# Coarse keys as 126 + 18 from the second batch on: four transposes instead of six, the rest keys of three groups in one

## The chip, the cores and the metric

The kernel runs on one core of a Trainium2 chip. The metric is the device time of one launch in microseconds (us). A NeuronCore has five engines that run side by side, each through its own instructions in order: TensorE (PE in the profile, its weight loads PEld), VectorE (DVE), ScalarE (ACT), GpSimd (POOL) and SyncE (SP, which here only issues DMAs). PE reads SBUF and writes PSUM; ACT and DVE read PSUM; POOL can't. Each DMA is issued from an engine's instruction stream, here from SP or POOL, and an engine that waits before a DMA holds back all that stands behind it in its stream.

## The reference

Inputs q, k, v are [8 batches, 8 heads, 576 positions, 64], in fp32. Two attentions are added, and the sum goes through a gated convolution and an output matrix:

```
# coarse: every 4 neighbouring positions are averaged, 576 -> Sd = 144 queries and keys
q_d = q.reshape(B, H, Sd, factor, D).mean(axis=3)      # k_d, v_d alike
out_d = sm_attn(q_d, k_d, v_d)                         # softmax over all 144 coarse keys
out_up = np.repeat(out_d, factor, axis=2)
# local: softmax over |i - j| < 4
attn_out = out_up + out_local
# then x = attn_out as [8, 576, 512]:
gate_pre = sum over 5 taps of conv_w[k] * x shifted    # causal, per channel
out = (sigmoid(gate_pre) * (x @ w_val)) @ w_out
```

## The kernel before

The heads are taken in pairs, so there are 32 of them: pair p is batch p // 4 and head pair p % 4 (two heads of 64 fill 128 partitions). For each pair PE makes, by their names in the profile:

- `mk`, `sl`: the local scores of ten blocks of 58 queries (L719 adds the band mask, L732 makes 40 small products), then a softmax on DVE and ACT (`mx`, `ex`, `sm`, `rs`, `pexp`).
- `sd`: the coarse scores (L809). They lie as three groups of 48 queries, [112 rows, 3 groups, 144 keys], the two heads at rows 0 to 47 and 64 to 111. From pair 8 on the scores of two pairs are made at once. ACT makes the exponentials `pd` group by group (L832) with their sums, and one of DVE, POOL or ACT multiplies them by the reciprocal sums (L855 or L857).
- `tl0`, `tl1`: five transposes of the local weights (L889), copied by ACT to `pt`.
- `tc0`, `tc1`: transposes of the coarse weights (L912). The 144 keys are cut in two halves of 72, and for each half the three groups are transposed, [112 x 72] to [72 x 112], into one PSUM tile: six transposes a pair. ACT copies each PSUM tile to `pdt` (L919), 72 x 336 values, twice a pair.
- `x`: local weights times values (L939, 20 products).
- `odp`: coarse weights times values (L981). From pair 4 on four products: for each half of the keys and each head, 72 keys by 64 columns of `vs` against 144 columns of `pdt`. ACT copies the result to `od` (L991), and DVE adds x and od to `xt` (L950).

From `xt` come the split into high and low parts (`xhs`, `xls`), and five taps of the convolution: ACT makes the first (L1024) into a buffer `gp`, DVE the other four (L1030), ACT the gate (L1041). There are GB = 7 buffers `gp`; the next user of one waits for the product `h` (L1147) that reads it.

The projections `val` and `out` run over blocks of 504 columns (all 4608 positions in a row), each in products of three fp32r passes (L1119 to L1121). They are cut into pieces of three matmuls (six in the last two half blocks) that a list calls P; they fill PE between the steps of the pairs. Eight P go with each pair in the steady order

```
STEADY = "odp'' x'' sd tc1' tc0' P P P P mk sl tl1' tl0' P P P P"
```

where two strokes mean the pair two steps back, and one stroke the pair before. A planner in the kernel takes every step with a cost, its dependencies and its buffers, and writes from that the order of each engine's instructions; it may take a step of the list up to 14 places early. Where it expects PE to idle, it puts matmuls on constants (L592) ahead of a step, to keep PE's clock up.

Values for `odp`: the four positions that make one coarse key are summed by DMAs. In the first batch `vg` comes in whole, and PE adds the four. From the second batch on `vs` is loaded from SP (`vs0`), and three DMAs on POOL add the rest (`vs1` to `vs3`, L634), each waiting for the one before. One such set serves the four pairs of a batch; up to four sets are held. VROWS = 80 rows of 4 KB go in each, of which 72 hold keys. The summed queries and keys `qs` come the same way from the third batch on.

DMAs on SP go through `send` (L609), which lets the fifth wait until the first of five has landed (PACE = 4). Work can move between DVE and POOL (and for the coarse normalization also ACT): the planner picks whichever is free.

Of the kernel before, what the change touches and what calls it, by code (L numbers as in the profile page):

```python
# [55 lines left out]
GB = 7  # L56
# [116 lines left out]
class Planner:  # L173
# [106 lines left out]
    def simulate(self):  # L280
# [97 lines left out]
        while len(start) < len(ops):  # L378
# [12 lines left out]
            for e in engines:  # L391
# [27 lines left out]
                if e == "SP":  # L419
                    flight.append(k)  # L420
# [67 lines left out]
def tensor_order(np_):  # L488
# [41 lines left out]
def tile_two_scale_attn_gated_conv(  # L530
# [6 lines left out]
    vgr: bass.AP,  # L537
    w_val: bass.AP,
# [24 lines left out]
    ods = [cpool.tile([P, SQ // 2], F32, name=f"od{i}") for i in range(2)]  # L563
    xhs, xls = (cpool.tile([P, NC, spot(LASTB * S) + S], F32R, name=n) for n in ("xhs", "xls"))
# [58 lines left out]
    def sums_in(b):  # L623
        u = bt.setdefault(b, {})

        def first(nm, src, shape):
            def run():
                u[nm] = inp.tile(shape, F32, tag=nm, name=f"{nm}{b}", bufs=VSB if nm == "vs" else 2)
                send(out=u[nm], in_=src[b, 0])
            return run  # L630

        def more(nm, src, r):
            def run():
                nc.gpsimd.dma_start(out=u[nm], in_=src[b, r], accum_op=ALU.add)  # L634
            return run

        for nm, src, shape, user, size in (
            ("qs", qkr, [P, NC, 2, SD], "sd", P * NC * 2 * SD * 4),
            ("vs", vgr, [VROWS, NC, 4, D], "odp", VROWS * NC * 4 * D * 4),
# [149 lines left out]
    def coarse_scores(p):  # L789
# [37 lines left out]
        def exp(g):  # L827
            def run():
                if g == 0:
                    s["pd"] = work.tile([ROWS, NG, SD], F32, tag="pd", name=f"pd{p}")  # L830
                    s["csm"] = small.tile([ROWS, NG], F32, tag="csm", name=f"csm{p}")
                nc.scalar.activation(  # L832
                    out=s["pd"][:, g],
# [18 lines left out]
        def norm(eng):  # L852
            if eng is nc.scalar:
                for g in range(NG):
                    nc.scalar.mul(s["pd"][:, g], s["pd"][:, g], s["crs"][:, g : g + 1])  # L855
                return
            return eng.tensor_tensor(  # L857
                out=s["pd"], in0=s["pd"], in1=s["crs"].broadcast_to([ROWS, NG, SD]), op=ALU.mult
# [43 lines left out]
    def coarse_transpose(p, kb):  # L902
# [3 lines left out]
        def mm():  # L906
# [4 lines left out]
            for i in range(NG):  # L911
                nc.tensor.transpose(  # L912
                    out=tp[:, i],
                    in_=s["pd"][:, i, half * kb : half * kb + half],
# [3 lines left out]
        def evac():  # L918
            nc.scalar.copy(out=s["pdt"][:, kb], in_=s["tc", kb])  # L919

        op(
            (f"tc{kb}", p), "PE", 295, mm, [("cnorm", p)],
            banks=[("t", [(f"pdt{kb}", p)])], cols=(588, 336), loads=3,
        )
        op((f"pdt{kb}", p), "ACT", 335, evac, [(f"tc{kb}", p)], free=[("odp", p - 2)])
# [425 lines left out]
```

## Time and profile before

| what | value |
|---|---|
| runs | 372.8, 372.87, 376.79 us (median 372.87) |
| the profiled execution's own time | 373.75 us |
| its span, first to last instruction | 371.5 us |
| mean granted TensorE clock | 0.999 |
| PE busy | 358.9 us (97%) |
| DVE busy | 304.9 us (82%) |
| ACT busy | 247.5 us (67%) |
| POOL busy | 91.1 us (25%) |
| bytes moved by DMA | 68.97 MB |

Busy time of PE counts a matmul until its result is written, so that matmuls that follow each other overlap, and a busy PE can still be waiting for weights. What a step costs PE is read from where the next one starts. An fp32 product shows as two matmuls (two passes), a transpose as one. Line numbers are those of the kernel before.

### The profile page before, as it was taken

The page shows a single profiled execution, that of the slowest core. Times are in us where ns is not written, and L with a number is a line of the kernel's source. Part 1 is how long each engine was busy: PE and PEld are TensorE (multiplying, and loading weights), DVE is VectorE, ACT ScalarE, POOL GpSimd, SP SyncE. Part 2 cuts the span into 40 slices and gives each one's busy share as a digit, 9 for nine tenths or more (in the row PEclk, how much of TensorE's full clock was granted, in tenths as well). Part 3 has the DMA queues.
Part 4 walks back from the last instruction along what each step waited for, and adds up shares of the span by engine and source line. Part 5 has one row for each costly group of instructions (what it writes and reads, how often), then busy time and mean ns, then how long its engine had stood idle before and what let it go on. Part 6 is the DMA issues. An engine that isn't in the chain of part 4 may idle for free.

```text
span 371.5 us, 14101 instructions
## 1 busy us (share of the span) xinstructions
PE 358.9 (97%) x6020; PEld 286.0 (77%) x6020; DVE 304.9 (82%) x673; ACT 247.5 (67%) x664; POOL 91.1 (25%) x116
## 2 busy tenths in 40 slices
PE   7899899998999999999999999999999999999996
PEld 4677676776777777777778787777777778778996
DVE  3988999998999989997999799879997999570520
ACT  2898798967875949674777587857874767422221
POOL 4211225741462116102522052203100320000000
PEclk9999999999999999999999999999999999999999
DMA  7899999999989969995799879892345101102012
GB/s 248 246 278 297 332 220 231 268 249 292 285 187 275 255 197 235 200 280 199 197 207 232 279 187 203 228 239 68 101 154 160 37 3 59 56 0 85 28 49 79
DMA packets 23550, 68.97 MB, mean 186 GB/s; under 512 B 2880, under 2 KB 8768, under 8 KB 23488
## 3 DMA queue, kind: packets, MB, share of 16 engines
q1 hardware_dynamic: 18592, 50.42, 42.0%
q0 software_dynamic: 4608, 17.50, 26.0%
q8 instruction: 47, 0.77, 0.9%
q10 hardware_dynamic: 288, 0.16, 0.2%
q14 instruction: 15, 0.12, 0.1%
HBM read 58.63 MB, written 9.44 MB: 183 GB/s over the span
## 4 chain that ended last, share of the span: by engine, by line
PE 75%; DMA 11%; DVE 9%; ACT 3%; issue 2%; POOL 0%; SPq 0%; DVEq 0%; ACTq 0%
PE val L1119 8%; PE val L1121 8%; PE val L1120 8%; PE out L1119 8%; PE out L1120 8%; PE out L1121 8%; DMA vg<-in_vg 6%; PE x L939 5%; PE sl L732 5%; PE odp L981 5%; PE tl L889 5%; PE tc L912 4%; DMA qk<-in_qk 3%; DVE gp L1030 3%; PE sd L809 3%; DMA out_t<-ob 2%
## 5 line engine op out<-in xcount | busy, mean ns | idle before, releaser
L1030 DVE SCALAR_TENSOR_TENSOR gp<-xt,cw,gp 128x576 f32<-128x576 f32 x128 | 106.0, 836 | 2.6 <-ACT gp L1024 2.4
L1119 PE MATMUL val<-xhs,wh_v 128*128 128x504 f32 (+1 forms) x160 | 63.2, 395 | 0.0
L1121 PE MATMUL val<-xls,wh_v 128*128 128x504 f32 (+1 forms) x160 | 59.6, 372 | 0.1
L1120 PE MATMUL val<-xhs,wl_v 128*128 128x504 f32 (+1 forms) x160 | 59.5, 372 | 0.0
L1119 PE MATMUL out<-hhl,wh_o 128*128 128x504 f32 (+1 forms) x144 | 57.6, 400 | 0.1
L1121 PE MATMUL out<-hhl,wh_o 128*128 128x504 f32 (+1 forms) x144 | 54.8, 380 | 0.0
L1120 PE MATMUL out<-hhl,wl_o 128*128 128x504 f32 (+1 forms) x144 | 54.7, 380 | 0.0
L1147 DVE SCALAR_TENSOR_TENSOR h<-gp,val 128x288 f32<-128x288 f32 (+6 forms) x64 | 26.7, 447 | 18.8 <-PE val L1121 18.5
L1211 ACT ACTIVATE ob<-out 128x504 f32<-128x504 f32 (+2 forms) x40 | 22.0, 551 | 24.7 <-PE out L1121 11.4
L832 ACT ACTIVATE pd<-sd,cbi 112x144 f32<-112x144 f32 x96 | 35.4, 380 | 1.6 <-DVE cbi L825 1.6
L1121 PEld LDWEIGHTS val<-xls,wh_v 128*128 128x128 f32 x160 | 30.1, 188 | 5.6 <-DVE xls L1013 0.5
L1119 PEld LDWEIGHTS val<-xhs,wh_v 128*128 128x128 f32 x160 | 30.1, 188 | 4.1 <-issue 0.2
L1120 PEld LDWEIGHTS val<-xhs,wl_v 128*128 128x128 f32 x160 | 30.2, 189 | 3.5
L1119 PEld LDWEIGHTS out<-hhl,wh_o 128*128 128x128 f32 x144 | 27.2, 189 | 5.8 <-issue 1.0
L1167 POOL TENSOR_TENSOR hhl<-h,hhl 128x504 fp32r<-128x504 f32 x15 | 19.2, 1278 | 49.9 <-DVE gp L1030 23.6
L1024 ACT ACTIVATE gp<-xt,cw 128x576 f32<-128x576 f32 x32 | 24.8, 776 | 9.5 <-DVE h L1147 7.4
L1121 PEld LDWEIGHTS out<-hhl,wh_o 128*128 128x128 f32 x144 | 27.1, 188 | 5.1
L1120 PEld LDWEIGHTS out<-hhl,wl_o 128*128 128x128 f32 x144 | 27.2, 189 | 3.8
L732 PEld LDWEIGHTS sl<-qk 64*29 64x29 f32 x2560 | 24.8, 103 | 6.9 <-issue 1.6
L1161 ACT CAST hhl<-h 128x504 fp32r<-128x504 f32 (+2 forms) x44 | 22.1, 521 | 11.9 <-DVE h L1147 11.9
L1009 ACT CAST xhs<-xt 128x576 fp32r<-128x576 f32 (+4 forms) x40 | 22.3, 577 | 11.7 <-DVE xt L950 11.4
L950 DVE TENSOR_TENSOR xt<-x,od 128x290 f32<-128x290 f32 x64 | 26.3, 450 | 4.6 <-PE x L939 3.3
(96 smaller groups left out, 731.5 us busy)
## 6 DMA issues: line engine op xcount, KB each, us to landing
qk<-in_qk SPq DMA_DIRECT2D x31, 586.0 KB, 5.6
qs<-in_qkr POOLq DMA_DIRECT2D x18, 576.0 KB, 7.9
vw<-in_vw SPq DMA_DIRECT2D x32, 320.0 KB, 5.9
out_t<-ob SPq DMA_DIRECT2D x32, 252.0 KB, 5.2
vs<-in_vgr POOLq DMA_DIRECT2D x21, 320.0 KB, 7.5
qs<-in_qkr SPq DMA_DIRECT2D x6, 576.0 KB, 7.4
vs<-in_vgr SPq DMA_DIRECT2D x7, 320.0 KB, 5.4
raw_v<-in_w_val SPq DMA_DIRECT2D x4, 512.0 KB, 6.0
```

The source lines that it names most:

```text
L732: nc.tensor.matmul(out=sc[32 * qd : 32 * qd + BQ, b, m * KW : (m + 1) * KW], lhsT=t[r, 0, 3 + blk : 3 + blk + BQ], rhs=t[r, 1, blk : blk + ...
L832: nc.scalar.activation(out=s["pd"][:, g], in_=s["sd"][:, g], func=AF.Exp, scale=1.0 / 128.0, bias=s["bi"][:, g : g + 1], accum_out=s["csm" ...
L950: nc.vector.tensor_tensor(out=s["xt"][:, 4:].rearrange("p (m a j r) -> p a m j r", m=NPR, a=2, r=2)[:, par], in0=s["x"][par].rearrange("p ...
L1009: nc.scalar.copy(out=xhs[:, c, g : g + t - f], in_=s["xt"][:, 4 + f : 4 + t])
L1024: nc.scalar.activation(out=s["gp"], in_=s["xt"][:, 4 : 4 + S], func=AF.Copy, scale=cw[:, c, 4:5])
L1030: return nc.vector.scalar_tensor_tensor(out=s["gp"], in0=s["xt"][:, k : k + S], scalar=cw[:, c, k : k + 1], in1=s["gp"], op0=ALU.mult, op1 ...
L1119: nc.tensor.matmul(out=o, lhsT=wh[:, d, col], rhs=his[d], start=d == 0, stop=False)
L1120: nc.tensor.matmul(out=o, lhsT=wl[:, d, col], rhs=his[d], start=False, stop=False)
L1121: nc.tensor.matmul(out=o, lhsT=wh[:, d, col], rhs=los[d], start=False, stop=d == NC - 1)
L1147: nc.vector.scalar_tensor_tensor(out=t["h"][:, cs], in0=st[b * NC + c]["gp"][:, f:e], scalar=1.0, in1=box["o"][:, cs], op0=ALU.add, op1=AL ...
L1161: nc.scalar.copy(out=t["hh"][:, cuts[n]], in_=t["h"][:, cuts[n]])
L1211: nc.scalar.mul(t["ob"][:, cs], box["o"][:, cs], 0.5)
```

## The change

For pairs 4 to 31 (the second to the last batch):

- ACT writes the exponentials interleaved, `pd` is [112, 144 keys, 3 groups], so that neighbouring keys of a group lie 12 bytes apart.
- The keys are cut into KM = 126 and KR = 18. Three transposes take the first 126 keys of each group ([112 x 126], read with the 12 byte step), and a fourth takes the last 42 keys of all three groups together, which lie in one run of 126 numbers. One PSUM tile [126, 4, 112] holds all, and one ACT copy of 126 x 448 takes it to `pdt`. The steps `tc0` and `tc1` become one, `tc1`.
- `odp` is two products of 144 columns (one a head) over 126 keys, and six of 48 columns (one a group and head) over the fourth transpose. For these, `vz` holds for each group the values of the 18 rest keys in the rows where that group's weights lie; its other rows are zero.
- `vs` is loaded as 126 rows of 2 KB. The 18 rest keys `vr` come beside it, in four further DMAs a batch (one from SP, three adding ones on POOL). `vz` is filled for each pair by three DMAs on SP from `vr`, 18 rows of 512 bytes each, which wait for the last sum `vr3` and for `odp` of the pair two before. Two `vz` buffers are zeroed once on POOL.
- GB goes from 7 to 6.

The first batch keeps its cut of 72 and 72, but its `pd` is interleaved too.

```diff
+KM, KR = 126, 18
+KW3 = KM // 3
-GB = 7
+GB = 6
...
+    vzs = [cpool.tile([KM, NG, 2, D], F32, name=f"vz{i}") for i in range(2)]
...
+            ("vs", vgr, [KM, 2 * NC * P], "odp", KM * NC * P * 4),
+            ("vr", vrr, None, "odp", KR * NC * P * 4),
...
+    def spread(p):
+        b, c = divmod(p, NC)
+
+        def dma(i):
+            def run():
+                nc.sync.dma_start(
+                    out=vzs[p % 2][KM - NG * KR + i : KM : NG, i].rearrange("k h d -> k (h d)"),
+                    in_=bt[b]["vr"][:, P * c : P * c + P],
+                )
+            return run
+
+        for i in range(NG):
+            op((f"vz{i}", p), "SP", 620, dma(i), [("vr3", b), ("vzero", 0)], free=[("odp", p - 2)], size=KR * P * 4)
...
-                    s["pd"] = work.tile([ROWS, NG, SD], F32, tag="pd", name=f"pd{p}")
+                    s["pd"] = work.tile([ROWS, SD, NG], F32, tag="pd", name=f"pd{p}")
...
-                    out=s["pd"][:, g],
+                    out=s["pd"][:, :, g],
...
+        def mm4():
+            s["pdt"] = work.tile([KM, NG + 1, ROWS], F32, tag="pdt", name=f"pdt{p}")
+            s["tc"] = tp = ps.tile([KM, NG + 1, ROWS], F32, tag="t", name=f"tc{p}", bufs=TB)
+            keep_warm(tp.rearrange("p a b -> p (a b)"))
+            for i in range(NG):
+                nc.tensor.transpose(
+                    out=tp[:, i],
+                    in_=s["pd"][:, 0:KM, i],
+                    identity=(ident_s if crossed(p, i) else ident)[0:ROWS, 0:ROWS],
+                )
+            nc.tensor.transpose(out=tp[:, NG], in_=s["pd"][:, SD - KW3 :].rearrange("p k i -> p (k i)"), identity=ident[0:ROWS, 0:ROWS])
+
+        def evac4():
+            nc.scalar.copy(out=s["pdt"], in_=s["tc"])
...
+                for h, r in enumerate((LO, HI)):
+                    nc.tensor.matmul(
+                        out=od_ps[r].rearrange("p (i j) -> p i j", j=GR),
+                        lhsT=vd[:, h],
+                        rhs=s["pdt"][:, 0:NG, 64 * h : 64 * h + GR],
+                        start=True,
+                        stop=False,
+                    )
+                for i in range(NG):
+                    for h, r in enumerate((LO, HI)):
+                        x = 64 * (1 - h if crossed(p, i) else h)
+                        nc.tensor.matmul(
+                            out=od_ps[r, GR * i : GR * i + GR],
+                            lhsT=vzs[p % 2][:, i, h],
+                            rhs=s["pdt"][:, NG, x : x + GR],
+                            start=False,
+                            stop=i == NG - 1,
+                        )
```

The planner gets costs for the new steps and writes a new order for every engine.

On PE, in the middle of the run (pair 21; `odp`, `x` and `tc` as above, `val` and `out` are pieces of the projections), there stands before:

```order
L1121 MATMUL val_3_4148<-xls,wh_v 128x504
L981 MATMUL odp_4185<-pdt_4032,vs_2608 64x144 x4
L939 MATMUL x_4193<-pt_4135,vw_3685 64x58 x20
L912 MATMUL tc_1_4221<-ident_s,pd_4062 72x112
L912 MATMUL tc_1_4221<-ident,pd_4062 72x112 x2
L912 MATMUL tc_0_4228<-ident_s,pd_4062 72x112
L912 MATMUL tc_0_4228<-ident,pd_4062 72x112 x2
L1119 MATMUL out_0_4234<-hhl_0_3967,wh_o 128x504
```

and now, at the same place:

```order
L1186 MATMUL val_3_4229<-xls,wh_v 128x504
L1026 MATMUL odp_4268<-pdt_4130,vs_2459 64x144 x2
L1036 MATMUL odp_4268<-pdt_4130,vz_90 64x48 x6
L986 MATMUL x_4282<-pt_4216,vw_3793 64x58 x20
L951 MATMUL tc_4308<-ident_s,pd_4213 126x112
L951 MATMUL tc_4308<-ident,pd_4213 126x112 x2
L956 MATMUL tc_4308<-ident,pd_4213 126x112
L1184 MATMUL out_0_4320<-hhl_0_4058,wh_o 128x504
```

The steps stand as they stood; four products became two wide and six narrow ones, and six transposes became four.

On SP, where the values of the second batch are first needed (`qk_1138` and `qk_1220` belong to pair 8, `vw_1151` and `vw_1169` to pair 7, `vs_1039` and `vs_1043` to the third batch), there stands before:

```order
L609 DMA qs_957<-in_qkr 128x1152
L609 DMA vw_1011<-in_vw 128x640
L609 DMA vs_1039<-in_vgr 80x1024
L609 DMA qk_1138<-in_qk 128x1172
L609 DMA vw_1151<-in_vw 128x640
L609 DMA qk_1267<-in_qk 128x1172
L609 DMA vs_1287<-in_vgr 80x1024
L609 DMA vw_1344<-in_vw 128x640
L609 DMA qk_1397<-in_qk 128x1172
```

and now (`vz_89` and `vz_90` are the two `vz` buffers, and `vs_604` the second batch's values):

```order
L615 DMA vs_1043<-in_vgr 126x512
L615 DMA vs_1067<-in_vgr 126x512
L667 DMA vz_89<-vs_604 18x128
L615 DMA vw_1169<-in_vw 128x640
L667 DMA vz_89<-vs_604 18x128 x2
L667 DMA vz_90<-vs_604 18x128 x3
L615 DMA vs_1043<-in_vrr 18x512
L615 DMA qk_1220<-in_qk 128x1172
L615 DMA vs_1067<-in_vrr 18x512
L667 DMA vz_89<-vs_604 18x128 x3
L667 DMA vz_90<-vs_604 18x128 x3
L615 DMA qk_1380<-in_qk 128x1172
```

The loads of pair 8 and 9 (`qk_1220`, `qk_1380`) now stand behind the spreading DMAs of pairs 4 to 7.

On DVE, around the `xt` of pair 4 (`xt_85<-x_1117` before, `xt_85<-x_1134` now; `gp` are taps of pairs 2 and 3), there stands before:

```order
L821 TENSOR_REDUCE cmx_1192<-sd_1162 112x3
L950 TENSOR_TENSOR xt_85<-x_1117,od_87 128x5x58 x2
L825 TENSOR_SCALAR cbi_1210<-cmx_1192 112x3
L769 TENSOR_TENSOR pexp_81<-ex_83,rs_1187 64x2x5x35
L1030 SCALAR_TENSOR_TENSOR gp_851<-xt_86,cw,gp_851 128x576
L1030 SCALAR_TENSOR_TENSOR gp_1058<-xt_84,cw,gp_1058 128x576
```

and now:

```order
L846 TENSOR_REDUCE cmx_1203<-sd_1175 112x3
L794 TENSOR_TENSOR pexp_81<-ex_83,rs_1200 64x2x5x35 x2
L1165 TENSOR_TENSOR wl_o<-a_o_1128,wh_o 128x512
L1095 SCALAR_TENSOR_TENSOR gp_855<-xt_86,cw,gp_855 128x576
L1095 SCALAR_TENSOR_TENSOR gp_1063<-xt_84,cw,gp_1063 128x576
L1095 SCALAR_TENSOR_TENSOR gp_855<-xt_86,cw,gp_855 128x576
L850 TENSOR_SCALAR cbi_1246<-cmx_1203 112x3
L1095 SCALAR_TENSOR_TENSOR gp_1063<-xt_84,cw,gp_1063 128x576
L1095 SCALAR_TENSOR_TENSOR gp_855<-xt_86,cw,gp_855 128x576
L1095 SCALAR_TENSOR_TENSOR gp_1063<-xt_84,cw,gp_1063 128x576
L997 TENSOR_TENSOR xt_85<-x_1134,od_87 128x5x58 x2
L1232 TENSOR_TENSOR hhl_0_1248<-h_0_1072,hhl_0_1248 128x504
```

The `xt` of pair 4 went behind six taps, and a `wl_o` and the second half of `pexp` came to DVE from POOL.

More of the change, by code (lines that the diff above doesn't have):

```diff
@@ L418, in simulate @@
                 heapq.heappush(wake, free[e])
-                if e == "SP":
+                if e == "SP" and not k[0].startswith("vz"):
                     flight.append(k)
@@ L508, in some @@
         key = (name, scored(p) if name == "sd" else p)
+        if name == "tc0" and p >= NC * FIRSTB:
+            return
         if 0 <= p < np_ and key not in seq:
@@ L627, in run @@
             def run():
-                u[nm] = inp.tile(shape, F32, tag=nm, name=f"{nm}{b}", bufs=VSB if nm == "vs" else 2)
-                send(out=u[nm], in_=src[b, 0])
+                if nm == "vr":
+                    u[nm] = u["vs"][0:KR, NC * P :]
+                else:
+                    u[nm] = inp.tile(shape, F32, tag=nm, name=f"{nm}{b}", bufs=VSB if nm == "vs" else 2)
+                send(out=u[nm][:, 0 : NC * P] if nm == "vs" else u[nm], in_=src[b, 0])
             return run
@@ L633, in run @@
             def run():
-                nc.gpsimd.dma_start(out=u[nm], in_=src[b, r], accum_op=ALU.add)
+                t = u[nm][:, 0 : NC * P] if nm == "vs" else u[nm]
+                nc.gpsimd.dma_start(out=t, in_=src[b, r], accum_op=ALU.add)
             return run
@@ L919, in evac @@
             nc.scalar.copy(out=s["pdt"][:, kb], in_=s["tc", kb])
[L921 to L925, printed above, removed]
+        def mm4():
[11 more added lines that the diff above has]
+            nc.scalar.copy(out=s["pdt"], in_=s["tc"])
+        if p < NC * FIRSTB:
+            op(
+                (f"tc{kb}", p), "PE", 295, mm, [("cnorm", p)],
+                banks=[("t", [(f"pdt{kb}", p)])], cols=(588, 336), loads=3,
+            )
+            op((f"pdt{kb}", p), "ACT", 335, evac, [(f"tc{kb}", p)], free=[("odp", p - 2)])
+        elif kb:
+            op(
+                ("tc1", p), "PE", 391, mm4, [("cnorm", p)],
+                banks=[("t", [("pdt1", p)])], cols=(784, 350), loads=4,
+            )
+            op(("pdt1", p), "ACT", 430, evac4, [("tc1", p)], free=[("odp", p - 2)])
     def local_av(p):
@@ L996, in coarse_av @@
         op(
-            ("odp", p), "PE", 543 if p >= NC * FIRSTB else 2010, mm,
-            [("vg", p) if p < NC * FIRSTB else ("vs3", p // NC), ("pdt0", p), ("pdt1", p)],
-            banks=[("t", [("od", p)])], cols=(648, 144), loads=8 if p >= NC * FIRSTB else 32,
+            ("odp", p), "PE", 583 if p >= NC * FIRSTB else 2010, mm,
+            [("vg", p) if p < NC * FIRSTB else ("vs3", p // NC)] + [(n, p) for n in ("vz0", "vz1", "vz2", "pdt0", "pdt1")],
+            banks=[("t", [("od", p)])], cols=(648, 144), loads=16 if p >= NC * FIRSTB else 32,
         )
@@ L1237, in out_unit, with vzero @@
         op((f"od{c}", j), "SP", 620, dma(slice(0, split), send), [(f"ob{c}", j)], size=P * split * 4)
+    def vzero():
+        return [nc.gpsimd.memset(t, 0.0) for t in vzs]
     def cw_in():
@@ L1254, in tile_two_scale_attn_gated_conv @@
         weight_chunk(q, "vo"[q // NC], (w_val, w_out)[q // NC], q % NC)
+    op(("vzero", 0), "POOL", 1000, vzero, port=("POOL",))
     for p in range(NP):
         load(p)
+        if p >= NC * FIRSTB:
+            spread(p)
         pool(p)
```

24 lines of the change are left out of this document (14 added, 10 removed).

## The prediction

> **What bounds the kernel now.** First the page: span, busy time of each engine.
>
> ```profile
> span 371.5 us, 14101 instructions
> PE 358.9 (97%) x6020; PEld 286.0 (77%) x6020; DVE 304.9 (82%) x673; ACT 247.5 (67%) x664; POOL 91.1 (25%) x116
> ```
>
> 97% says little, since it is an average over stages. So next the windows, cut at the `odp` of pair 8 and at the last `odp`, and one window inside the first stage (each row: window, its length, busy time of PE, PEld, DVE, ACT, POOL, then granted clock, DMA share and GB/s).
>
> ```profile
> 0.00:98.27 98.27, 89.23 (x1732) 66.62 (x1732) 87.48 (x199) 78.47 (x210) 33.60 (x56) 1.00 0.97 267
> 98.27:318.50 220.23, 220.23 (x3956) 174.88 (x3957) 199.94 (x442) 154.35 (x425) 57.50 (x60) 1.00 0.70 183
> 318.50:371.50 53.00, 49.45 (x336) 44.45 (x336) 17.50 (x33) 14.66 (x31) 0.00 (x0) 0.99 0.14 47
> 40.00:80.00 40.00, 37.25 (x632) 28.62 (x629) 39.65 (x85) 37.05 (x94) 19.32 (x23) 1.00 0.98 261
> ```
>
> Up to 98 us PE has gaps (89.2 of 98.3), and between 40 and 80 DVE works 39.65 of 40 us: there DVE sets the pace, with ACT at 37.05 and the DMA engines near it. From 98.27 to 318.5 PE is busy without a gap, and every step saved or added on PE counts in full. After 318.5 comes the end of the projections, which the change doesn't touch. The clock is 1.00 throughout.
>
> Last the chain of waits (start, duration, engine, tile, line, count), for the price of one step in the middle stage, with the fully fed `odp` of the first batch for comparison.
>
> ```profile
> 44.27 2.11 PE odp L981 x32
> 98.34 0.64 PE odp L981 x8
> 201.07 0.70 PE tl L889 x5
> 205.13 0.74 PE x L939 x40
> 205.87 0.70 PE tc L912 x6
> 318.50 0.64 PE odp L981 x8
> ```
>
> From the first to the last of these `odp` are 23 pairs: (318.50 - 98.34)/23 = 9.57 us a pair, with 24 `odp` and 23 sets of transposes.
>
> **The change on PE, middle stage: products.** An `odp` of 32 passes takes 2.11 us, one of 8 takes 0.64: (2.11 - 0.64)/24 = 0.061 a pass. A product is two passes, 0.1225, the four of a pair come one after the other, and 0.64 - 4 x 0.1225 = 0.15 is the entry. `x` has 20 products of 58 columns, which run two at a time, since each head needs only half of the array's rows: ten steps of two passes, (0.74 - 0.15)/10 = 0.059, although by columns alone they would be 58/144 x 0.1225 = 0.049. After: two products of 144 columns (one a head, over 126 keys) in place of four, 0.245, and six of 48, which with 126 keys fill the rows and so come one by one. A narrow one is between 48/144 x 0.1225 = 0.041 and the 0.059 of a step of `x`, to which it is nearest (same 64 weight columns, ten columns fewer). I take 0.059 for five and 0.041 for the last, behind which nothing is fed: 0.15 + 0.245 + 5 x 0.059 + 0.041 = 0.73, against 0.64: **+0.09 a pair**, between 0.00 and +0.11.
>
> **Transposes.** The timeline of PE around one pair:
>
> ```profile
> 204.42 0.71 PE L981 MATMUL odp<-pdt,vs 72*64 72x144 f32 x8
> 205.06 0.81 PE L939 MATMUL x<-pt,vw 64*64 64x58 f32 x40
> 205.80 0.29 PE L912 MATMUL tc<-ident_s,pd 112*72 112x112 f32 x1
> 205.92 0.35 PE L912 MATMUL tc<-ident,pd 112*72 112x112 f32 x2
> 206.12 0.26 PE L912 MATMUL tc<-ident_s,pd 112*72 112x112 f32 x1
> 206.21 0.36 PE L912 MATMUL tc<-ident,pd 112*72 112x112 f32 x2
> 206.34 0.47 PE L1119 MATMUL val<-xhs,wh_v 128*128 128x504 f32 x1
> ```
>
> From 205.92 to 206.21 are three steps: 0.097 each, with 72 weight columns and 112 moving. Two go: -0.193. The weights grow to 126 columns. The loads, grouped:
>
> ```profile
> L889 PEld LDWEIGHTS tl<-ident,pexp 128*128 128x128 f32 x160 | 17.5, 141 | 4.5 <-ACT pdt L919 1.2 <-POOL half L698 0.6 <-ACT gp L1041 0.5
> L912 PEld LDWEIGHTS tc<-ident,pd 112*72 112x72 f32 x104 | 11.2, 115 | 0.6 <-ACT pd L855 0.2
> ```
>
> 128 columns take 141 ns, 72 take 115: +0.025 for the first load, which nothing hides. The others lie under the moving stream: in `x` each pass has its own load and a step of 0.059 holds two passes after each other, so a 64-column load takes at most 0.0295, 0.46 ns a column, 58 ns for 126, well under 97. Together **-0.168 a pair** (down to -0.193 if the first load too is hidden).
>
> The Trainium skill ("TensorE: Matmul & The Clock Gate", section on LDWEIGHTS) prices a load at its columns over 1.2, in ns: 105 for 126 columns, more than the moving stream. By it three steps would be 0.008 longer and the middle stage 0.6 us worse; the trace speaks against it, since 64 columns would take 53 ns where `x` shows at most 29.5.
>
> The new loads read `pd` at 12 byte steps, which no row of before shows. Bounds: no loss; or a third of the rate (the rival below). I take no loss.
>
> Middle stage: 23 x -0.168 = -3.9, 24 x +0.09 = +2.2; **-1.7 us** (ends -4.4 and -1.2).
>
> **ACT, DVE and DMA in the middle stage.** ACT is at 154/220 = 70% there.
>
> ```profile
> L832 ACT ACTIVATE pd<-sd,cbi 112x144 f32<-112x144 f32 x96 | 35.4, 380 | 1.6 <-DVE cbi L825 1.6
> L919 ACT COPY pdt<-tc 72x336 f32<-72x336 f32 x64 | 25.1, 433 | 6.3 <-PE tc L912 5.6
> ```
>
> Two copies of 433 ns become one of 448 columns, 433 to 433 x 448/336 = 577: 0.29 to 0.43 less a pair. The strided exponentials, 3 x 380, cost nothing (they are read from PSUM as before) to, at double, 1.1 more, which ACT would still hold. So nothing on the path; what hides it is PE's 9.57 a pair, and without that cover it would be a gain. DVE, at 91%, takes over what POOL did: it stays just under. In the middle stage `vz` has a whole pair's 9.57 us for 27 KB behind `odp` of two pairs back, on SP, ahead of loads that run pairs ahead of their use: nothing.
>
> **The first stage.** DVE sets it, so what counts is the work DVE has done before the `xt` of pairs 8 to 10. The order moves work on DVE; the rows for its price:
>
> ```profile
> L1030 DVE SCALAR_TENSOR_TENSOR gp<-xt,cw,gp 128x576 f32<-128x576 f32 x128 | 106.0, 836 | 2.6 <-ACT gp L1024 2.4
> L769 DVE TENSOR_TENSOR pexp<-ex,rs 64x350 f32<-64x350 f32 x51 | 27.8, 545 | 1.1
> L857 DVE TENSOR_TENSOR pd<-pd,crs 112x432 f32<-112x432 f32 x11 | 6.6, 603 | 0.1
> L698 DVE TENSOR_TENSOR half<-qk 128x288 f32<-128x288 f32 x7 | 3.2, 452 | 6.6 <-DMA qk<-in_qk 6.5
> L699 DVE TENSOR_TENSOR qs<-half 128x144 f32<-128x144 f32 x12 | 3.6, 300 | 0.0
> L1167 DVE TENSOR_TENSOR hhl<-h,hhl 128x504 fp32r<-128x504 f32 x9 | 6.0, 671 | 0.7 <-ACT hhl L1161 0.7
> L1100 DVE TENSOR_TENSOR wl_o<-a_o,wh_o 128x512 fp32r<-128x512 f32 x2 | 1.3, 653 | 0.0
> ```
>
> Ahead of the `xt` of pair 10 DVE has, against before, two `wl_o` (1.31), three `pexp` (1.64), one `half` (0.45) and one `pd` (0.60) more, one `qs` (0.30) and one `hhl` (0.67) fewer: +3.0; and three taps (2.51) fewer, which stand behind it now: +0.5. The same count is +1.6 at pair 9 and, with four taps and two `cmx` put off, -1.8 at pair 8. I take **+0.7**, ends -1.8 and +3.0. The added matmuls on constants stand where PE has gaps anyway.
>
> **Sum.** -1.7 + 0.7 = -1.0 on the profiled execution, 373.75 (span 371.5 and 2.25 around it): 372.75. The median is 0.88 below that execution, so **371.9**. With one term at its end at a time the sum runs from -4.4 + 0.7 = -3.7 and -1.7 - 1.8 = -3.5 to -1.2 + 0.7 = -0.5 and -1.7 + 3.0 = +1.3; some of both low ends together gives -5. So 367.9 to 374.2 is its own range.
>
> **Rivals.** *Slower: the detour of the rest keys.* Until now `odp` of pair 4 waited for three sums on POOL; now for `vr3`, issued behind them, and then a second transfer on SP. The page's transfers (count, KB each, median us from issue to landing), then the timeline, its POOL, PE and DVE rows:
>
> ```profile
> vs<-in_vgr POOLq DMA_DIRECT2D x21, 320.0 KB, 7.5
> vw<-in_vw SPq DMA_DIRECT2D x32, 320.0 KB, 5.9
> out_t<-ob SPq DMA_DIRECT2D x7, 144.0 KB, 1.8
> ...
> 35.16 0.96 POOL L634 DMA_DIRECT2D vs<-in_vgr  x1 [10.62 <-DVE pd L857]
> 43.74 0.82 POOL L634 DMA_DIRECT2D vs<-in_vgr  x1 [1.58 <-DMA vs<-in_vgr]
> 51.95 0.81 POOL L634 DMA_DIRECT2D vs<-in_vgr  x1 [3.72 <-DVE gp L1030]
> 57.41 0.71 PE L981 MATMUL odp<-pdt,vs 72*64 72x144 f32 x8
> 64.83 0.71 PE L981 MATMUL odp<-pdt,vs 72*64 72x144 f32 x8
> 59.47 0.82 DVE L950 TENSOR_TENSOR xt<-x,od 128x290 f32<-128x290 f32 x2
> 60.98 3.72 DVE L1030 SCALAR_TENSOR_TENSOR gp<-xt,cw,gp 128x576 f32<-128x576 f32 x5
> ```
>
> The sums start at 35.16, 43.74 and 51.95, and the `odp` follows 5.5 after the last. I put `vr3` behind them, issued about 53 and landed at 57 to 59 (an estimate from those 5.5). The three `vz` take then between the 1.8 of the smallest transfer and the 5.9 of one on SP: 59 to 65. The order has room for that: this `odp` stands where the next one stood (64.83), and on DVE its `xt` stands behind six taps (6 x 0.74, from 3.72/5), a `wl_o` and one more `pexp`: 59.47 + 4.5 + 0.65 + 0.55 = 65.2, and with a `wl_o`, a `half` and a `pexp` moved ahead of those, 1.65, 66.8. From `odp` to `xt` it was 59.47 - 57.41 = 2.1. So the detour decides if this `odp` starts after 64.7; from there DVE stands still, and every us is one at the end, as a DVE at 39.65 of 40 has none to give back. Behind the waiting `vz` on SP stand the loads of pairs 8 and 9, so that their `sl` is late as well. A landing at 69.7 costs 5 us: **377**. For it: POOL must issue in time between its own work, and the DMA share is 0.97. Against: small transfers, and room of 6 us over the earliest landing. Chance of such a price 0.14; up to 1 us of it lies in my range.
>
> *Slower: the strided weights.* If 12 byte steps load at a third of the rate, 126 columns take 3 x 58 = 174 ns: the first load costs 0.141 over the 72-column one of 33, the two behind it 0.077 each over 0.097, so the transposes come to -0.193 + 0.141 + 0.154 = +0.10 a pair: 23 x 0.10 + 2.2 + 0.7 = +5.2, **378**. At half the rate (116) it is -0.193 + 0.083 + 0.038 = -0.07, sum +1.2, inside my range. Against: nothing shows either way. Chance 0.05 for the third. The Trainium skill ("SBUF — State Buffer", note on cachelines) asks for two accesses to each 16 byte line for full rate; at 12 bytes there are 1.33, which would be two thirds, 87 ns: still under 0.097, and the sum 0.7 us worse.
>
> *Faster: narrow steps at their columns.* At 0.041 each `odp` is 0.64, +2.2 falls away, and with -1.8 from the first stage the sum is -3.9 - 1.8 = -5.7: **367.2**. For it: nothing but columns distinguishes the two prices. Against: `x` at 0.059 for 58. Chance 0.21.
>
> *Slower: six buffers for taps.* A tap waits for `h` of a block back; PE has 9.57 a pair, DVE 91%. If DVE falls a pair behind at each of the later blocks, some +4 at most: 376. Chance 0.04.
>
> **How the numbers follow.** Forecast 0.56, and the four rivals 0.14, 0.05, 0.21, 0.04. About 1% is what a measurement of this kernel can tell from no change: 3.7 us, so faster is under 369.1, slower over 376.6. Faster: the 0.21, and 0.01 of the forecast's low end. Slower: 0.14 and 0.05, with 0.01 of the six buffers. The rest, 0.58, is within. The range goes from 367.6 to 377.0, leaving out half of the fast rival and the strided one.
>
> **What would show it.** After: the `odp` in the chain at 0.73, the four transposes at 0.53, a period of 9.49 between `odp`s, ACT's copy at 433 to 577. A transpose step over 0.10 speaks for the strided weights; `odp` at 0.64 for the fast rival. Right in the first stage would be the `odp` of pair 8 near 99.0 (96.5 to 101.3 with its ends); wrong, DVE idle with `xt` behind an `odp` of pair 4 that starts after 64.7, its wait being `vz`.

## The result

| | runs | median, us | lowest to highest | ratio to before, 95% interval |
|---|---|---|---|---|
| before | 22 | 375.57 | 372.37 to 378.41 | |
| after | 22 | 378.69 | 375.06 to 381.25 | 1.0084 [1.0057, 1.0111] |

The changed kernel is 0.84% slower, where 0.26% faster was forecast (371.9 on 372.87). 378.69 also lies outside the range (367.6 to 377.0). Part of that distance is the base: the three runs of before that were shown had a median of 372.87, the 22 beside the changed kernel 375.57. Only the ratio is free of this.

The profiled execution of after took 375.06 us, the lowest of its 22, against 373.75 before. Its page:

```profile
span 373.3 us, 14602 instructions
PE 359.7 (96%) x6201; PEld 291.2 (78%) x6201; DVE 309.3 (83%) x680; ACT 245.0 (66%) x639; POOL 103.0 (28%) x131
```

Cut at the same places as before (the `odp` of pair 8 and the last one; columns as in the prediction):

```profile
0.00:97.91 97.91, 88.75 (x1742) 67.71 (x1743) 86.31 (x196) 74.22 (x192) 38.14 (x64) 1.00 0.93 253
97.91:320.26 222.35, 221.32 (x4117) 178.89 (x4116) 202.74 (x448) 154.78 (x415) 64.88 (x67) 1.00 0.71 187
320.26:373.30 53.04, 49.63 (x345) 44.62 (x344) 20.30 (x37) 15.96 (x32) 0.00 (x0) 1.00 0.14 48
```

The first stage seems a little shorter (97.91 against 98.27), the middle one 2.1 us longer (222.35 against 220.23), the end equal. But the first cut misleads: the order puts other work ahead of the `odp` of pair 8 than before (24 matmuls of `sd` fewer). At pair 9 the same 48 pieces of the projections lie behind PE in both. Three profiles of each kernel (two of each come from the runs below) give:

| us | before | after | difference of the means |
|---|---|---|---|
| start to the `odp` of pair 9 | 107.57, 106.51, 104.67 | 107.96, 109.43, 108.33 | +2.3 |
| `odp` of pair 9 to that of pair 12 | 29.01, 28.79, 28.92 | 29.73, 29.96, 29.37 | +0.8 |
| `odp` of pair 12 to that of pair 31 | 181.84, 182.01, 183.19 | 182.57, 182.58, 183.60 | +0.6 |
| `odp` of pair 3 to that of pair 12 | 92.39, 91.43, 91.23 | 93.81, 94.26, 93.75 | +2.3 |
| DVE busy from pair 3 to pair 12 | 87.1, 86.3, 86.3 | 87.8, 89.3, 87.9 | +1.8 |

In the second profile of after PE's clock was halved for 3.41 us near 20 us; without that profile the first difference is +1.9. The last two rows start behind it. For the first profile of each they come from these windows:

```profile
44.20:136.59 92.39, 89.42 (x1602) 69.25 (x1600) 87.09 (x191) 71.86 (x196) 34.09 (x39) 1.00 0.98 256
43.88:137.69 93.81, 89.76 (x1661) 71.29 (x1659) 87.77 (x192) 67.96 (x182) 39.85 (x46) 1.00 0.96 247
```

So most of what the first stage loses stands beside more work on DVE: three `pexp`, two `wl_o` and one `pd` more in this stretch, against three taps, one `qs` and one `hhl` fewer, in all three profiles.

Most of the whole is lost before pair 12, and the steady stage, where 1.7 us were to be gained, loses a little. Why the gain is missing is seen on PE, around one pair in that stage:

```profile
128.38 0.47 PE L1026 MATMUL odp<-pdt,vs 126*64 126x144 f32 x4 [0.46 <-ACT pt L919]
128.67 0.51 PE L1036 MATMUL odp<-pdt,vz 126*64 126x48 f32 x12
129.11 0.81 PE L986 MATMUL x<-pt,vw 64*64 64x58 f32 x40
129.84 0.36 PE L951 MATMUL tc<-ident_s,pd 112*126 112x112 f32 x1
130.04 0.39 PE L951 MATMUL tc<-ident,pd 112*126 112x112 f32 x2
130.27 0.26 PE L956 MATMUL tc<-ident,pd 112*126 112x112 f32 x1
130.30 0.47 PE L1184 MATMUL val<-xhs,wh_v 128*128 128x504 f32 x1
```

From the start of `odp` to that of `x` it is 129.11 - 128.38 = 0.73, as forecast (0.64 before). From the first transpose to `val` it is 130.30 - 129.84 = 0.46, against 206.34 - 205.80 = 0.54 before: 0.08 less, not 0.17. The first step takes 0.20, the next two 0.23 together, 0.115 each, where 0.097 had been expected.

### The profile page after: what moved, and what is told of

It reads as the page before. It is cut to its first block, busy times and chain, and to the rows that moved or that the text cites. A ratio compares the mean times of both kernels' runs of the same rounds, so it can differ in the third digit from the quotient of the medians.

```text
span 373.3 us, 14602 instructions
## 1 busy us (share of the span) xinstructions
PE 359.7 (96%) x6201; PEld 291.2 (78%) x6201; DVE 309.3 (83%) x680; ACT 245.0 (66%) x639; POOL 103.0 (28%) x131
## 4 chain that ended last, share of the span: by engine, by line
PE 71%; DMA 11%; DVE 7%; ACT 6%; issue 2%; POOL 1%; SPq 1%; ACTq 0%; POOLq 0%; DVEq 0%
PE out L1184 8%; PE out L1186 8%; PE out L1185 8%; PE val L1184 7%; PE val L1186 7%; PE val L1185 7%; PE sl L757 5%; PE x L986 5%; PE tl L914 4%; PE tc L951 3%; DMA vs<-in_vrr 3%; PE odp L1026 3%; DVE gp L1095 2%; PE sd L834 2%; PE odp L1036 2%; DMA vg<-in_vg 2%
## 5 line engine op out<-in xcount | busy, mean ns | idle before, releaser
L1095 DVE SCALAR_TENSOR_TENSOR gp<-xt,cw,gp 128x576 f32<-128x576 f32 x128 | 104.3, 829 | 0.1
L1186 PE MATMUL val<-xls,wh_v 128*128 128x504 f32 (+1 forms) x160 | 59.6, 372 | 0.6 <-DVE xls L1078 0.6
L857 ACT ACTIVATE pd<-sd,cbi 112x144 f32<-112x144 f32 x96 | 38.8, 462 | 14.2 <-DVE cbi L850 14.0
L1232 POOL TENSOR_TENSOR hhl<-h,hhl 128x504 fp32r<-128x504 f32 (+1 forms) x17 | 23.8, 1460 | 49.8 <-DVE rs L788 17.5
L794 DVE TENSOR_TENSOR pexp<-ex,rs 64x350 f32<-64x350 f32 x56 | 32.3, 577 | 1.3
L644 POOL DMA_DIRECT2D vs<-in_vrr x21 | 21.3, 1014 | 33.5 <-DMA vs<-in_vrr 24.0
```

What stands on the lines that cost most here:

```text
L794: return eng.tensor_tensor(out=px[r].rearrange("p (m b) k -> p b m k", b=2)[:, :, :, BQ * e : BQ * e + KW], in0=s["ex"][r].rearrange("p (b ...
L857: nc.scalar.activation(out=s["pd"][:, :, g], in_=s["sd"][:, g], func=AF.Exp, scale=1.0 / 128.0, bias=s["bi"][:, g : g + 1], accum_out=s["c ...
L1095: return nc.vector.scalar_tensor_tensor(out=s["gp"], in0=s["xt"][:, k : k + S], scalar=cw[:, c, k : k + 1], in1=s["gp"], op0=ALU.mult, op1 ...
L1186: nc.tensor.matmul(out=o, lhsT=wh[:, d, col], rhs=los[d], start=False, stop=d == NC - 1)
L1232: return eng.tensor_tensor(out=t["hl"][:, cs], in0=t["h"][:, cs], in1=t["hh"][:, cs].bitcast(F32), op=ALU.subtract)
```

## The experiments

Three theories to begin with. **A**: loads of weights at a step of 12 bytes set the step of the transposes. **B**: the detour of the rest keys (`vr3`, then `vz`, then `odp`) is late at run time. **C**: six tap buffers are too few. The first four runs shared one chip. "Order" is that of the instructions on every engine.

**The yardstick.** The changed kernel again.

> The changed kernel once more, beside its variants, as their yardstick. All theories: 0.6 to 1.1% over the kernel before; per pair from the odp of pair 11 to that of pair 31 about 9.59 us against 9.56 before, transposes 0.46 a pair.

1.0093 [1.0055, 1.0131]: as at first.

**Contiguous loads and exponentials.**

```diff
-                in_=s["pd"][:, 0:KM, i],                 # pd [112, 144 keys, 3 groups]
+                in_=s["pd"][:, i, 0:KM],                 # pd [112, 3 groups, 144 keys]
-  in_=s["pd"][:, SD - KW3 :].rearrange("p k i -> p (k i)")
+  in_=s["pd"].rearrange("p i k -> p (i k)")[:, NG * SD - KM :]
```

> The exponentials lie group by group again, and all four transposes read runs of 126 neighbours; the fourth takes 126 numbers that are not the rest keys of all groups, so the rest weights of two groups are other numbers. Order of all engines as in the changed kernel. Theory A (12 byte loads set the transpose step): the loads fall from 196 to 209 ns to about 157, the transposes from 0.46 to 0.37 a pair as forecast, 20 pairs take 1.9 us less, the whole 2.6 less, ratio to before 1.000 to 1.003; and if the slower strided exponentials (462 against 380 ns) held up the stretch up to 128 us, another 1 us. Theory B (detour of the rest keys) and C (six tap buffers): the middle stage as in the changed kernel, ratio still 1.006 to 1.010.

**Contiguous loads alone.**

```diff
-                    in_=s["pd"][:, 0:KM, i],
+                    in_=s["pd"].rearrange("p k i -> p (k i)")[:, KM * i : KM * (i + 1)],
```

> The exponentials are written interleaved as in the changed kernel, but the first three transposes read runs of 126 neighbours, so they transpose other numbers (the three groups mixed). Only PE's loads change. Theory A: transposes 0.37 a pair, 2.6 us less in all, exponentials still 462 ns. If ACT's exponentials are the cost instead: as the changed kernel in the stretch up to 128 us, and gained only what the loads give. Theories B and C: no change beyond 0.3 us.

Loads alone: 1.0007 [0.9976, 1.0037], 0.86% under the yardstick, 3.2 us. PE in its profile:

```profile
132.58 0.31 PE L951 MATMUL tc<-ident_s,pd 112*126 112x112 f32 x1
132.73 0.35 PE L951 MATMUL tc<-ident,pd 112*126 112x112 f32 x2
132.92 0.26 PE L956 MATMUL tc<-ident,pd 112*126 112x112 f32 x1
132.95 0.48 PE L1184 MATMUL val<-xhs,wh_v 128*128 128x504 f32 x1
```

From 132.58 to 132.95 it is 0.37: what the prediction had for the transposes. The first step fell from 0.20 to 0.15, the next two from 0.115 to 0.095 each. Grouped, the loads of after, and then of this run:

```profile
L951 PEld LDWEIGHTS tc<-ident,pd 112*126 112x126 f32 x44 | 7.7, 209 | 0.0
L956 PEld LDWEIGHTS tc<-ident,pd 112*126 112x126 f32 x28 | 4.4, 157 | 0.0
```

```profile
L857 ACT ACTIVATE pd<-sd,cbi 112x144 f32<-112x144 f32 x96 | 38.9, 463 | 13.2 <-DVE cbi L850 13.0
L951 PEld LDWEIGHTS tc<-ident,pd 112*126 112x126 f32 x44 | 5.5, 140 | 0.1
```

209 ns at a step of 12 bytes, 140 side by side. The exponentials, at 463, are as slow as in after, so that ACT's part of the interleaving isn't what set the step. Theory A holds for the step of the transposes: 28 pairs of 0.09 are 2.5 of the 3.2 us.

The other run also has 0.37 a pair and exponentials of 384 ns, and yet gives 1.0066 [1.0029, 1.0104]. PE's waits between 98 and 325 us in its profile (us in total, times, longest):

```profile
PE tl L914 <- DVE pexp L794: 2.0, 2, 1.4
PE out L1184 <- DVE h L1212: 1.1, 2, 0.8
PE sl L757 <- issue: 0.6, 1, 0.6
```

It waited 3.1 us for DVE; the profile of the loads alone has 2.0 us of waits there, none of them for DVE (1.7 for `hhl` of POOL). The two intervals overlap (up to 1.0037, from 1.0029). Whether faster exponentials really made DVE late stays open; no gain from them shows. The shorter step is in both traces, its whole worth in the time only in the run of the loads alone.

**No wait for the detour, same order.** The spreading DMAs read the first position of the rest keys from HBM. The adding DMAs are still issued on POOL, but nothing reads what they sum.

```diff
-                    in_=bt[b]["vr"][:, P * c : P * c + P],
+                    in_=vrr[b, 0][:, P * c : P * c + P],
```

> The three spreading DMAs of a pair read the first addend of the rest keys straight from HBM, so they no longer wait for the last sum vr3; the sums of the rest keys over four positions are left out. Order as in the changed kernel. Theory B: the odp of pair 4 starts near 57 instead of 62.6, the loads for pairs 8 and 9 go out some us earlier, the odp of pair 11 comes 1 to 1.5 us earlier and the whole ends as much earlier, ratio 1.004 to 1.006; middle stage unchanged. Theory A: at most 0.3 us less, since DVE sets the first stage whatever the odp of pair 4 waits for.

1.0079 [1.0044, 1.0115]: hardly less than the yardstick. The `odp` of pair 4 came later, not earlier:

```profile
67.82 0.47 PE L1026 MATMUL odp<-pdt,vs 126*64 126x144 f32 x4
68.11 0.51 PE L1036 MATMUL odp<-pdt,vz 126*64 126x48 f32 x12
```

It no longer waits for `vz`. In after it did, in the midst of its own products:

```profile
63.88 0.69 PE L1036 MATMUL odp<-pdt,vz 126*64 126x48 f32 x8 [0.71 <-DMA vz<-vs]
```

This wait is 0.7 us in two of the three profiles of after and absent in the third, and without it the kernel lost as much. So theory B, as a wait at run time, fell. What delayed this execution stood further up, in the waits of DVE and of PE between 46 and 56 us, behind which PE's clock was halved from 52.8 to 59.6 us:

```profile
DVE qs L724 <- POOL half L723: 3.9, 1, 3.9
...
PE val L1186 <- DVE xls L1078: 3.9, 1, 3.9
```

In front of that `half` on POOL stands an adding DMA, and POOL's waits before such DMAs in after are long:

```profile
POOL vs L644 <- DMA vs<-in_vrr: 24.0, 8, 8.3
POOL vs L644 <- DMA vs<-in_vgr: 11.8, 9, 2.8
```

Hence theory **D**: the adding DMAs of the rest keys hold POOL back, and through `half` and `hhl` DVE and PE.

**No adding DMAs for the rest keys** (their sums left out), alone and with contiguous loads; and **each of them right behind the other of the same position**, with nothing left out. All in the order of after.

```diff
             def run():
+                if nm == "vr":
+                    return
                 t = u[nm][:, 0 : NC * P] if nm == "vs" else u[nm]
                 nc.gpsimd.dma_start(out=t, in_=src[b, r], accum_op=ALU.add)
+                if nm == "vs":     # only in the third of these runs
+                    nc.gpsimd.dma_start(out=u["vr"], in_=vrr[b, r], accum_op=ALU.add)
```

> The three adding DMAs of the rest keys of each batch are not issued on POOL (the rest keys are summed over one position instead of four); vz then waits for vr0 alone. Order otherwise as in the changed kernel. Theory D (POOL waits at these DMAs for landings, holds back the half and qs that DVE needs, and later hhl that PE needs): DVE's wait before qs near 50 us goes, the odp of pair 11 comes 1 to 3 us earlier than in the changed kernel, the waits of PE in pairs 9 and 19 shrink, whole 1.5 to 3 us less, ratio 1.001 to 1.005. Theory B and A alone: at most 0.5 us less.

> The last two edits together: no adding DMAs for the rest keys, and the first three transposes read runs of 126 neighbours (other numbers). Order as in the changed kernel. Theories A and D, if they add: 2.6 us and 1.5 to 3 us less than the changed kernel, ratio 0.993 to 0.998, pairs 11 to 31 in 190.0 us. If D is wrong: as the edit of the loads alone, 1.000 to 1.002.

> Nothing is left out: each DMA of the rest keys is issued right behind the DMA of the other keys that adds the same position, so that both landings pass during one wait of POOL. The other instructions keep their order. Theory D: POOL's waits fall by about 20 us, the wait of DVE near 50 us mostly goes, whole 1 to 2 us less than the changed kernel, ratio 1.003 to 1.006. If the DMA traffic itself costs, and not the waits of POOL: as the changed kernel, 1.008 to 1.010.

1.0061 [1.0018, 1.0104], 1.0080 [1.0040, 1.0120] and 1.0225 [1.0164, 1.0287]. In these times nothing that D asked for came, and the last, meant as a mend, is the worst of all. Its windows show what goes on (PE's clock is the third number from the end):

```profile
44.00:48.00 4.00, 3.09 (x42) 2.77 (x43) 2.98 (x8) 3.85 (x12) 0.86 (x2) 0.86 1.00 288
48.00:52.00 4.00, 4.00 (x55) 2.86 (x52) 2.39 (x10) 1.54 (x4) 1.50 (x3) 0.50 0.90 324
...
72.00:76.00 4.00, 0.92 (x5) 0.57 (x6) 1.43 (x4) 1.71 (x4) 3.36 (x6) 0.77 0.99 184
76.00:80.00 4.00, 4.00 (x22) 2.75 (x21) 2.83 (x9) 1.02 (x3) 2.98 (x4) 0.50 0.91 190
```

PE waited 1.9 us at first and then 3.7. Each time its clock was halved for 6.8 us, and the stage loses on both. The second wait has no releaser in the profile; it stands in the middle of a group of products:

```profile
70.59 0.79 PE L992 MATMUL x<-pt,vw 64*64 64x58 f32 x37
75.08 0.47 PE L992 MATMUL x<-pt,vw 64*64 64x58 f32 x3 [3.70 <-issue]
```

The run without adding DMAs has one there as well (2.57 us). So these runs came out with halved clocks in 10, 11 and 6 of 12, 12 and 6 executions, and their medians say little on POOL itself. At a granted clock of 0.998 or more two executions of the first are left, 375.35 and 375.64 us, where the median of after at such clocks is 377.31 (16 executions of three timings); and one of the second, 374.13, where the loads alone have 374.99 (7 executions, all these on other chips). The profile of the second is that one. From the `odp` of pair 3 to that of pair 12 it shows

```profile
45.79:137.52 91.73, 88.86 (x1661) 70.55 (x1659) 86.58 (x192) 67.69 (x182) 30.69 (x35) 1.00 0.97 251
```

This is as short as in the kernel before (91.2 to 92.4, in after 93.8 to 94.3), with the order of after; shorter transposes can have given up to 0.7 of it. That speaks for D, from very few executions: D is neither shown nor excluded.

**The kernel before, profiled and timed.** Theory **E**: what after loses in the first stage are such halvings, which its order makes more frequent.

> The kernel before, profiled once more, to see how far one profile of it differs from another. All theories: pairs 11 to 31 in 191.1 to 191.4 us; the odp of pair 11 within 1 us of 127.3 if the first stage repeats itself, up to 4 us later if its loads land unevenly from run to run, as the profiles of the changed kernel suggest (128.4 and 130.1).

> The kernel before, timed like the others, so that the granted clock of each of its runs is listed too. Theory E (what decides the first stage is whether PE waits long enough there for its clock to be halved for 3.4 us, and the changed order makes such waits more frequent): most runs of the kernel before have a clock of 0.998 or more, against 8 of 22 of the changed kernel, and its runs at full clock lie 1.5 to 2.5 us under those of the changed kernel. If the clock dips come by chance alike in both: as many low clocks as in the changed kernel, about two in three.

b0 took 372.63 us, with the `odp` of pair 11 at 125.77 (127.27 in the profile shown, 124.28 in the next): the first stage of one and the same kernel differs by up to 3 us from profile to profile, for a cause that no run here shows. b1: 1.0009 [0.9975, 1.0042] to the other runs of the same kernel. 6 of its 12 executions had a granted clock below 0.998, of after 13 of 22. Over all executions of these two kernels whose clock is listed beside a run it was 57 of 144 before and 30 of 46 after: halvings are more frequent in after, as E has it. But they aren't what after loses: of the executions at 0.998 or more the median is 374.38 before (b1) and 377.29 after (374.41 and 377.31 over all), 2.9 us apart with the clock full in both. So E fell as the account of the loss.

**The change from the third batch on.** Pairs 4 to 7 as before, in the order written anew; then with contiguous loads.

```diff
-        if p < NC * FIRSTB:        # transposes, products, values, spreading
+        if p < NC * NEWB:          # NEWB = 2; in the second run also in_=...[:, KM * i : KM * (i + 1)]
```

> The change from the third batch on (pairs 8 to 31); the second batch (pairs 4 to 7) is computed as before, with its values as 80 rows and six transposes. Theory E: the stretch up to the odp of pair 8 is as in the kernel before (97 to 99), few clock dips, pairs 11 to 31 as in the changed kernel (191.9); whole 1.5 to 3 us under the changed kernel, ratio to before 1.001 to 1.004. If the loss of the first stage comes from the later batches' DMAs on POOL or SP: ratio 1.006 to 1.010 as the changed kernel.

> As the run before, and the first three transposes read runs of 126 neighbours (other numbers). Theories A and E together: pairs 11 to 31 in 190.0 to 190.2, 2 us under the run before, ratio to before 0.995 to 0.999. If A's gain is lost elsewhere: no better than the run before.

1.0015 [0.9977, 1.0052] and 0.9972 [0.9936, 1.0009]. With pairs 4 to 7 as before, 0.8% is gone, some 2.9 us (the yardstick stood on another chip); the contiguous loads give 0.4% more, less than the intervals can tell.

**Six tap buffers in the kernel before** (`GB = 6`).

> The kernel before with six tap buffers in place of seven, nothing else (the planner writes its order anew). Theory C: 1.5 to 3 us slower than before, ratio 1.004 to 1.008, with DVE or ACT waiting for h. All others: 0.998 to 1.002.

0.9993 [0.9963, 1.0024]. Theory C fell.

Beside D there is theory **F**: the planner knows of the detour, expects the rest keys late, and writes an order around that, in which `odp` of pair 4 stands behind 16 pieces instead of 10, next to that of pair 5. The next two ask this from both sides, with the changed kernel on the same chip.

> The changed kernel, as the yardstick beside the next two. All theories: ratio to before 1.006 to 1.011.

1.0093 [1.0054, 1.0132].

**No detour in the second batch, order anew.** The rest keys of pairs 4 to 7 come unsummed, straight from HBM; that batch's own load and three adding DMAs for them go with it.

```diff
-                    in_=bt[b]["vr"][:, P * c : P * c + P],
+                    in_=vrr[b, 0][:, P * c : P * c + P] if b == 1 else bt[b]["vr"][:, P * c : P * c + P],
-   op((f"vz{i}", p), "SP", 620, dma(i), [("vr3", b), ("vzero", 0)], ...
+   op((f"vz{i}", p), "SP", 620, dma(i), [("vr3", b)] * (b > 1) + [("vzero", 0)], ...
```

> In the second batch alone (pairs 4 to 7) the rest keys come straight from HBM, one position instead of the sum of four, and the order of all engines is written anew with that: the odp of pair 4 moves back from 16 to 8 pieces of the projections, apart from that of pair 5. Theory F (the first stage is lost by the order written around the detour): the odp of pair 11 near that of the kernel before, whole 2 to 3 us under the changed kernel, ratio 1.000 to 1.003. If the products and transposes themselves, or the DMAs of later batches, cost the first stage: as the changed kernel, 1.006 to 1.011.

1.0014 [0.9981, 1.0047], 0.8% under the changed kernel, and the two intervals don't meet. The two `odp` have parted again:

```profile
56.63 0.47 PE L1026 MATMUL odp<-pdt,vs 126*64 126x144 f32 x4 [0.17 <-ACT pdt L959]
56.93 0.50 PE L1036 MATMUL odp<-pdt,vz 126*64 126x48 f32 x12
67.34 0.47 PE L1026 MATMUL odp<-pdt,vs 126*64 126x144 f32 x4
67.64 0.50 PE L1036 MATMUL odp<-pdt,vz 126*64 126x48 f32 x12
```

**The detour alone, in the kernel before.** Its four DMAs a batch and three a pair are added, into a tile that nothing reads, and `odp` waits for them.

```diff
+            ("vr", vrr, None, "odp", KR * NC * P * 4),
+            op((f"vz{i}", p), "SP", 620, dma(i), [("vr3", b)], free=[("odp", p - 2)], size=KR * P * 4)
+                    if p in vzd:
+                        behind(mm1, vzd.pop(p))
-GB = 7
+GB = 6
```

> The kernel before (four products, six transposes, exponentials group by group) with the detour alone: the rest keys are loaded and summed in four further DMAs a batch and spread by three DMAs a pair, as in the change, into a tile that nothing computes with, and odp waits for them; six tap buffers, for the room. The order comes out with the odp of pair 4 behind 16 pieces, next to that of pair 5, as in the changed kernel. Theory F: the first stage is lost here too, 2 to 3 us, ratio 1.005 to 1.009, pairs 12 to 31 as before. Otherwise: 0.999 to 1.002.

1.0120 [1.0066, 1.0174], with pairs 12 to 31 as before (182.07 against 181.84). Here the `odp` of pair 4 really waits, 4.4 us, and holds `xt` up. All six executions had a granted clock of 0.991 or less, and in the profiled one it was halved for 6.8 us at this wait:

```profile
PE odp L1000 <- DMA vz<-vrt: 5.0, 2, 4.4
```

```profile
DVE xt L969 <- ACT od L1012: 2.9, 1, 2.9
```

So the detour in the second batch costs the first stage, with or without the new products, and it goes when that batch is spared it, although the new transposes and products stay. By which way it costs in after is not settled. It isn't PE's wait for `vz`: that is 0.7 us at most there, and the run that took only this wait away kept the loss. The order written around the detour (F) and the adding DMAs on POOL (D) remain. Sparing the second batch the detour changes both at once; the detour alone in the kernel before adds a wait of 4.4 us to both; and the few executions at full clock without the adding DMAs, in the order of after, speak for D. The order by itself, with nothing else changed, was not tried.

**Contiguous loads with the right numbers.** From the third batch on, exponentials group by group; a copy lays the last 42 weights of the three groups side by side.

```diff
+        def rest(eng):
+            s["pr"] = stage.tile([ROWS, KM], F32, tag="bits", name=f"pr{p}", bufs=1)
+            return eng.tensor_copy(out=s["pr"]..., in_=s["pd"][:, :, SD - KW3 :])
```

> The change from the third batch on, nothing left out: the exponentials lie group by group, three transposes read runs of 126 keys, and a copy on DVE or POOL puts the last 42 weights of the three groups side by side for the fourth. If theories A and F are the whole account: transposes 0.37 a pair, pairs 12 to 31 in 180.8 to 181.5 us, ratio to before 0.994 to 0.999. If the copy costs on DVE, which is busy 91% there, more than it gives: 1.000 to 1.005, with PE waiting for DVE.

1.0009 [0.9972, 1.0046]. The transposes fall to 0.37 a pair (6.94 us from pair 12 to 31, against 8.74), but that stretch takes 183.56 us. In place of the saving stand waits of PE, here from 98 us on:

```profile
PE sl L759 <- issue: 1.5, 2, 0.8
PE sd L836 <- issue: 1.0, 1, 1.0
PE x L995 <- issue: 0.4, 1, 0.4
```

The copies took 276 ns on DVE and 290 on POOL, and no wait for them shows. The waits above, 1.9 us of them between pairs 12 and 31, have no releaser in the profile, and there are such waits in that stretch without any copy: 1.2 us in the third profile of before, 1.05 in the third of after. They don't make up the whole difference, so why the saving doesn't show here is open. No version here is faster than the kernel before by more than its interval.

## Why the prediction was wrong

- **What bounds what**: right in the main. PE sets the middle stage (busy 221.3 of 222.4 us), and before it DVE has little to spare (87.8 of 93.8 us from pair 3 to pair 12). The 0.09 us a pair that contiguous loads take from PE were found again from pair 12 to 31 in two profiles with the order of after (180.87 and 180.83 us, in after 182.57 to 183.60), but not in three others (182.78, 182.63 and 183.56).
- **Products, +0.09 a pair**: right, to the hundredth (0.64 to 0.73; 20 pairs from 12.82 to 14.60 us, 1.78/20 = 0.089). The narrow product costs as a step of `x` does, 0.059, so the fast rival (0.041) fell.
- **Transposes, -0.168 a pair**: the first step that failed, by the sentence "I take no loss" for loads at 12 byte steps. 20 pairs fell from 10.68 to 9.20 us, 0.074 each. That is the half rate which the text had priced at -0.07 among the rivals and put aside for want of a row. The run with contiguous loads, 0.37 a pair, shows that it is the step of 12 bytes. The chosen value cost 23 x 0.09 = 2.1 us of the forecast, and by itself turned -1.7 in the middle stage into +0.4.
- **The two rules of the Trainium skill.** The Trainium skill ("TensorE: Matmul & The Clock Gate", LDWEIGHTS) would have contiguous loads of 126 columns at 105 ns, an estimate by its rule; the trace disagrees, as the prediction said, since steps of 0.095 held them. The cacheline note of the Trainium skill ("SBUF — State Buffer") points the right way for the strided ones, but by two thirds of the rate, an estimate from it, they would be 87 ns and hidden; the steps of 0.115 fit half the rate (116).
- **ACT and DVE in the middle stage**: right. The single copy takes 539 ns (433 to 577 given), the exponentials 462 instead of 380, and no wait of PE for them shows. Not forecast were PE's waits from 98 us on, 1.0 us in the profile of after: 0.5 for `pexp` of DVE and 0.5 for `pt` of ACT.
- **The first stage, +0.7**: the second step that failed, and it was mis-sized. The runs show 2.9 us that go with the detour of the second batch, near the upper end that the text gave (+3.0). That DVE's work is what counts was right. Its count came to -1.8, +1.6 and +0.5 at the three cuts (pairs 8, 9 and 10), and +0.7 was taken; the last cut took three taps set behind it as 2.51 us saved. Measured, DVE works 1.8 us more from pair 3 to pair 12, with three taps fewer, and the stretch is 2.3 us longer.
- **The rival of the detour** had the right part of the change, and the wrong point from which it decides. The text let it cost only if `odp` of pair 4 started after 64.7. It started at 62.61, 63.97 and 63.67 in the three profiles of after, and the time was lost all the same. So the 0.14 was set on a late landing, while the detour costs by another way, the order or the adding DMAs on POOL.
- **Six tap buffers**: right to be thought little of (0.9993).
- With both steps as measured in the experiments the sum is -1.7 + 2.1 + 2.9 = +3.3 us on 375.57, 0.9%, against 0.84% measured.

## What to carry to other kernels

Where a layout makes an engine read at a new step, and no row of the trace shows such a read, "no loss" is the end of a range and not its middle: price it between the bounds, or measure one such instruction first. Here it was half the rate. A value that arrives by one more hop can cost without a wait for it: the order and the extra DMAs that come with the hop have a price too, and it doesn't show among the waits for the value. Which of the two it was here is not shown. A saving on the busiest engine must be looked for in the whole time: 0.09 us a pair came back whole in two profiles, and in three others PE had waits in its place, for DVE, for ACT, or with no releaser.

## What the runs showed of the hardware

- PE's clock was halved for 3.41 or 6.83 us during waits of PE or within 2 us behind them. In the profiles here, up to the last `odp`, this came with all four waits of 2.57 to 4.39 us, and with 5 of 13 waits of 1.46 to 1.97 us. 57 of 144 executions of the kernel before and 30 of 46 of after had a clock below 0.998. One stretch of 3.41 us at half clock is 3.41/2 in 372 us, 0.0046 of the mean clock, and the listed clocks come in such steps (0.995, 0.991, 0.986). The Trainium skill ("TensorE: Matmul & The Clock Gate", on the clock gate) speaks of an idle window of about 3.4 us; waits shorter than that were enough here, as one of 1.46 us ahead of a halving.
- PE can stop for 2.6 to 3.7 us inside a group of equal products, with no releaser in the profile. In both profiles a load of the queue called instruction had ended about 1.2 us before PE went on (70.6 and 71.8 us; 73.8 and 75.1), which would fit late instructions; this was not tested, and with 48 such loads in 381 us two near ones can be chance.
- Each adding DMA of the rest keys right behind the other of its position, so that POOL should wait less, made the kernel 1.3% slower than the changed one (on another chip). All six executions had clocks of 0.978 to 0.989; the cause of the rest wasn't found.
